# A fused linear-attention and MLP kernel: doubled powers of w taken one step later, w's column through ScalarE's queue, 11 dummies, the last copy in two halves

## The chip, the cores and the metric

The kernel runs on one core of a Trainium2 chip. The metric is device microseconds of one launch; lower is better. The time before is the median of three runs.

## The reference

Two steps follow one another. The first is a linear attention with a decaying state (4 batches, 8 heads, 768 positions, head width 48), the second an MLP with an unusual activation over the 3072 tokens:

```python
for t in range(S):
    cur = einsum('bhd,bhe->bhde', u[None] * k[t], v[t])
    y[:, :, t] = einsum('bhd,bhde->bhe', r[t], state + cur)
    state = w[None, :, :, None] * state + einsum('bhd,bhe->bhde', k[t], v[t])
x = y.transpose(0, 2, 1, 3).reshape(B * S, H * D)   # 3072 x 384
h = x @ w_in                                        # 384 x 2048
g = h * erf(softplus(h))
return g @ w_out                                    # 2048 x 384
```

## The kernel before

**Tiling.** The 768 positions of a batch are cut in chunks of 128, 24 chunks in all; four chunks make a block of 512 tokens, and there are six blocks. Inside a chunk the decay is taken out of the recurrence by scaling r with rising powers of w and k with falling ones, so that the chunk's scores are one matrix product A, masked, and the state is carried on by products with w to the 128th. The MLP then works on a block of 512 tokens and 128 hidden columns at a time: 96 steps (h, activation, output sum). Matrix products of the MLP are done in three pieces, high and low parts of both operands.

**Order.** Nothing is left to a scheduler. A string ORDER of short words is walked from left to right (lines 549 to 619), and each word issues one step on its engines: L loads a chunk, B builds the tables of powers (L179 to L185), J multiplies a chunk by them (L228), A is the score product (L317), V turns k (L249 to L261), P masks (L328), Y and D are the output and the state products (L346, L369), f and p the two MLP products (L425, L485), a to l the steps of the activation, O the output (L497 to L514), Z0a, Z0b and Z0c a count of columns of w that lie outside 0.7 to 0.97. An engine takes its instructions in this order and stands still when one has to wait.

**The start.** SyncE (SP) sends the loads; the first two are wc, w as a column (112 partitions by 4), and uc, the same for u (L77 to L80). The chunks' loads follow (L71, L75). VectorE clears a tile `warm`; ScalarE does one Tanh on it (L89), which loads its activation table; then TensorE does WARM = 16 dummy products of this tile into a spare accumulator (L95, L516, L719). Meanwhile VectorE makes the powers (L163 to L177): `wp[n]` is w to the 2^n (a square, L171) and its reciprocal (L172), and `pw` holds all powers from 0 to 63, doubled in length with each of six products (L176). The 64 powers times w to the 64th give the other half of the tables `wrk` (L184 on VectorE, plain copies on ScalarE, L182). The first chunk is multiplied by them at L230, and the first A follows. Pool clears and fills small tables beside it, `own` among them (L216 to L222), which takes w to the 128th.

**The count and the end.** The count's matmul (L527, two of 4 columns) sums flags in `bad`. A rare case of w outside its bounds is handled behind a branch on that count (L629 to L631), which every engine passes at the end. The last step's three output tiles (128 by 512 each) are copied out of their accumulators, tiles 0 and 2 by ScalarE (L506), tile 1 by VectorE (L504), and sent to memory by SP (L492), one transfer of 256 KB each.

Of the kernel before, what the change touches and what calls it, by code (L numbers as in the profile page):

```python
# [18 lines left out]
ALU = mybir.AluOpType  # L19
# [4 lines left out]
SHIFT = 256.0  # L24
# [5 lines left out]
P = 128  # L30
C = 128
D = 48
NPAIR = 4
PR = 112
NF = 16
NQ = 3
TB = 512
# [6 lines left out]
def body(ctx: ExitStack, tc: tile.TileContext, att, attn, wcol, ucol, u, win, wout, levels, outT):  # L44
    nc = tc.nc
# [31 lines left out]
    wc = const.tile([PR, NPAIR], F32, name="wc")  # L77
    nc.sync.dma_start(out=wc, in_=wcol)
    uc = const.tile([PR, NPAIR], F32, name="uc")
    nc.sync.dma_start(out=uc, in_=ucol)  # L80
    ub = const.tile([P, 384], F32, name="ub")
# [67 lines left out]
    H = C // 2  # L149
# [13 lines left out]
    wp = const.tile([PR, 8, 2, NPAIR], F32, name="wp")  # L163
# [3 lines left out]
    nc.gpsimd.memset(pw[:, 0, :, 0:1], 1.0)  # L167
    nc.vector.tensor_scalar(out=wp[:, 0, 0], in0=wc, scalar1=0.7, scalar2=0.97, op0=ALU.max, op1=ALU.min)
    for n in range(7):
        m = 1 << n  # L170
        nc.vector.tensor_tensor(out=wp[:, n + 1, 0], in0=wp[:, n, 0], in1=wp[:, n, 0], op=ALU.mult)  # L171
        nc.vector.reciprocal(out=wp[:, n, 1], in_=wp[:, n, 0])  # L172
        if n == 0:
            nc.vector.tensor_copy(out=pw[:, 1, :, 0], in_=wp[:, 0, 1])
        if n < 6:
            nc.vector.tensor_tensor(out=pw[:, :, :, m:2 * m], in0=pw[:, :, :, 0:m],  # L176
                                    in1=wp[:, n, :, :, None].to_broadcast([PR, 2, NPAIR, m]), op=ALU.mult)  # L177

    def tables(eng):  # L179
        for o, n in ((wr, 0), (wk, 1)):  # L180
            if eng is nc.scalar:
                nc.scalar.copy(out=o[:, :, 0:H], in_=pw[:, n])  # L182
            else:
                nc.vector.tensor_tensor(out=o[:, :, H:C], in0=pw[:, n],  # L184
                                        in1=wp[:, 6, n, :, None].to_broadcast([PR, NPAIR, H]), op=ALU.mult)  # L185
# [30 lines left out]
    own = const.tile([PR, NPAIR, 2], F32, name="own")  # L216
# [3 lines left out]
    nc.gpsimd.memset(top.rearrange("p n two -> p (n two)").bitcast(I32), 0)  # L220
    for r, hh in ((slice(0, D), 0), (slice(H, PR), 1)):
        nc.gpsimd.tensor_copy(out=own[r, :, hh], in_=wp[r, 7, 0])  # L222

# [264 lines left out]
    def put_out(n, e, blk=None):  # L488

        b = order[n][0]  # L490
        o = outT[b] if blk is None else outT[bass.ds(blk, 1)].rearrange("a p n -> (a p) n")
        nc.sync.dma_start(out=o[e * P:(e + 1) * P], in_=outs[n, e])  # L492

# [3 lines left out]
    def end(step, n, e):  # L497
        b, f = order[n]
        if step == "a":
            o = outs[n, e] = fp.tile([P, TB], F32, tag="s1" if n == NS - 1 and e == 2 else "o", name=f"o{n}_{e}")  # L500
            if (b, e) in part:
                nc.sync.dma_start(out=o, in_=part[b, e])
            elif b == NB - 1 and e == 1:
                nc.vector.tensor_scalar(out=o, in0=full[n, e], scalar1=SHIFT * SHIFT, scalar2=None, op0=ALU.mult)  # L504
            else:
                nc.scalar.mul(out=o, in_=full[n, e], mul=SHIFT * SHIFT)  # L506
# [42 lines left out]
    for i, x in enumerate(words):  # L549
# [22 lines left out]
        elif what == "B":  # L572
            tables(eng)
        elif what == "H":
            diagonals()
# [142 lines left out]

WARM = 16  # L719
LEAN = 8  # L720
# [55 lines left out]
l64 A23 p64x p64y a67 c66 d66 e66 b67 P230 P231 z67 g66 O631b O630b O632a p64z p65 f69 c67 h66 a68 b68 l66 S18c z68  # L776
c68 d68 e68 d67 e67 a69 g68 h68 g67 p66 Y23 Y22 X23a h67 X23b l68 X22a b69 X22b z69 l67 f70 f71 c69 d69 a70 b70 z70
e69 p67 c70 d70 a71 g69 b71 h69 l69 f72 a72 z71 c71 d71 e70 p68 p69 e71 g70 g71 h71 l71 b72 h70 z72 l70 f73 Z0b f74
p70 c72 a73 d72 e72 b73 a74 g72 Z0c z73 c73 h72 b74 d73 l72 p71 f75 O632b z74 e73 g73 c74 d74 h73 e74 a75 b75 g74 l73
# [78 lines left out]
```

## Time and profile before

| | us |
|---|---|
| median of three runs (500.76 to 502.0) | 500.99 |
| span of the profiled execution | 498.5 |
| TensorE (PE) busy in it | 489.1 |
| TensorE loading weights (PEld), beside it | 391.7 |
| ScalarE (ACT) busy | 390.6 |
| VectorE (DVE) busy | 334.2 |
| GpSimd (POOL) busy | 149.9 |

The profile gives the span of one execution, from its first to its last instruction; the runs' times take in what lies around it. Busy shares are averages over three stages: a start of some 8 us, the first attention chunks beside the fetching of weights, and the long stretch in which attention of later blocks and the MLP are woven together. TensorE is busy 98% of the span and makes up 92% of the chain of work that ended last, so the stages at both ends, where it is not busy, are to be read apart.

### The profile page before, as it was taken

The page shows a single profiled execution, that of the slowest core. Times are in us where ns is not written, and L with a number is a line of the kernel's source. Part 1 is how long each engine was busy: PE and PEld are TensorE (multiplying, and loading weights), DVE is VectorE, ACT ScalarE, POOL GpSimd, SP SyncE. Part 2 cuts the span into 40 slices and gives each one's busy share as a digit, 9 for nine tenths or more (in the row PEclk, how much of TensorE's full clock was granted, in tenths as well). Part 3 has the DMA queues.
Part 4 walks back from the last instruction along what each step waited for, and adds up shares of the span by engine and source line. Part 5 has one row for each costly group of instructions (what it writes and reads, how often), then busy time and mean ns, then how long its engine had stood idle before and what let it go on. Part 6 is the DMA issues. An engine that isn't in the chain of part 4 may idle for free.

```text
span 498.5 us, 10972 instructions
## 1 busy us (share of the span) xinstructions
PE 489.1 (98%) x4466; PEld 391.7 (79%) x4466; DVE 334.2 (67%) x584; ACT 390.6 (78%) x702; POOL 149.9 (30%) x132
## 2 busy tenths in 40 slices
PE   8999999999999999999999999999999999999995
PEld 4877888878778888888888878887878788888883
DVE  7999866667878966746766676786764544434552
ACT  2779999998976687877568875768877888978793
POOL 8749436016222735800067063361000000000000
PEclk9999999999999999999999999999999999999998
DMA  8965663328007603000440123231010000100001
GB/s 291 345 247 194 221 218 123 132 64 301 25 1 269 201 30 122 35 1 1 153 149 0 34 83 135 93 113 76 11 54 1 1 0 1 43 22 1 0 1 68
DMA packets 14136, 48.15 MB, mean 97 GB/s; under 512 B 1792, under 2 KB 2176, under 8 KB 14080
## 3 DMA queue, kind: packets, MB, share of 16 engines
q1 hardware_dynamic: 14080, 47.39, 26.8%
q8 instruction: 37, 0.61, 0.5%
q14 instruction: 19, 0.16, 0.1%
HBM read 41.09 MB, written 6.29 MB: 95 GB/s over the span
## 4 chain that ended last, share of the span: by engine, by line
PE 92%; DVE 4%; ACT 2%; issue 1%; DVEq 0%; ACTq 0%
PE h L425 39%; PE acc L485 39%; PE y L346 7%; PE A L317 4%; PE ds L369 1%; PE dummy L95 1%; DVE gl L468 1%; DVE am L325 1%; DVE s L457 1%; DVE s L441 1%; DVE wt L136 1%; PE kt L255 0%; ACT gh L463 0%; ACT L89 0%; ACT s L453 0%
## 5 line engine op out<-in xcount | busy, mean ns | idle before, releaser
L425 PE MATMUL h<-x,wih 128*128 128x512 f32 x576 | 182.8, 398 | 0.1
L425 PEld LDWEIGHTS h<-x,wih 128*128 128x128 f32 x576 | 107.1, 188 | 27.2 <-DVE s L457 0.6
L485 PE MATMUL acc<-gh,woh 128*128 128x512 f32 x288 | 115.2, 400 | 0.0
L485 PE MATMUL acc<-gl,woh 128*128 128x512 f32 x288 | 114.1, 396 | 0.3 <-DVE gl L468 0.2
L485 PE MATMUL acc<-gh,wol 128*128 128x512 f32 x288 | 113.9, 395 | 0.0
L425 PE MATMUL h<-x,wil 128*128 128x512 f32 x288 | 113.9, 395 | 0.0
L468 DVE TENSOR_TENSOR gl<-s,gh 128x512 fp32r<-128x512 f32 x96 | 71.3, 744 | 51.2 <-ACT gh L463 50.0
L457 DVE SCALAR_TENSOR_TENSOR s<-s,h 128x512 f32<-128x512 f32 x96 | 65.5, 684 | 49.0 <-ACT s L453 48.5
L441 DVE SCALAR_TENSOR_TENSOR s<-s,h 128x512 f32<-128x512 f32 x96 | 65.5, 685 | 34.8 <-ACT s L436 32.7
L445 ACT ACTIVATE s<-s 128x512 f32<-128x512 f32 x96 | 60.0, 626 | 23.5 <-DVE s L441 23.3
L432 ACT ACTIVATE s<-h 128x512 f32<-128x512 f32 x96 | 56.5, 590 | 26.5 <-PE h L425 26.2
L463 ACT CAST gh<-s 128x512 fp32r<-128x512 f32 x96 | 58.6, 613 | 20.5 <-DVE s L457 15.8
L485 PEld LDWEIGHTS acc<-gh,woh 128*128 128x128 f32 x288 | 54.1, 188 | 13.8 <-ACT s L445 0.2
L485 PEld LDWEIGHTS acc<-gl,woh 128*128 128x128 f32 x288 | 54.1, 188 | 13.7 <-DVE gl L468 1.2
L425 PEld LDWEIGHTS h<-x,wil 128*128 128x128 f32 x288 | 54.1, 188 | 13.0
L485 PEld LDWEIGHTS acc<-gh,wol 128*128 128x128 f32 x288 | 54.1, 188 | 12.9
L449 ACT ACTIVATE s<-s 128x512 f32<-128x512 f32 x96 | 60.3, 629 | 1.8
L436 ACT ACTIVATE s<-s 128x512 f32<-128x512 f32 x96 | 60.3, 629 | 1.7
L453 ACT ACTIVATE s<-s 128x512 f32<-128x512 f32 x96 | 60.0, 629 | 2.0
L536 POOL TENSOR_TENSOR att<-att,wrk 112x512 f32<-112x512 f32 x28 | 41.3, 1476 | 42.3 <-DMA att<-in_att_dram 39.9
L536 POOL TENSOR_TENSOR am<-idents,q 128x512 f32<-128x512 f32 x22 | 25.4, 1156 | 54.2 <-issue 24.3
L325 DVE COPY_PREDICATED am<-mask,A 64x128 f32<-64x128 uint32 (+2 forms) x108 | 38.0, 388 | 3.3 <-PE A L317 2.6
(88 smaller groups left out, 431.2 us busy)
## 6 DMA issues: line engine op xcount, KB each, us to landing
att<-in_att_dram SPq DMA_DIRECT2D x22, 608.0 KB, 5.6
att<-in_att_dram SPq DMA_DIRECT2D x24, 512.0 KB, 4.0
raw<-in_wout_dram SPq DMA_DIRECT2D x8, 768.0 KB, 5.6
raw<-in_win_dram SPq DMA_DIRECT2D x7, 768.0 KB, 4.7
out_dram<-o SPq DMA_DIRECT2D x18, 256.0 KB, 2.3
part<-o SPq DMA_DIRECT2D x6, 256.0 KB, 3.1
o<-part SPq DMA_DIRECT2D x6, 256.0 KB, 3.2
raw<-in_win_dram SPq DMA_DIRECT2D x2, 384.0 KB, 8.1
```

Of the source, the lines that this page charges most:

```text
L425: nc.tensor.matmul(out=h, lhsT=w[:, f, q, :], rhs=x[:, xi, q, :], start=k == 0, stop=k == 8)
L432: nc.scalar.activation(out=s1, in_=e["h"], func=AF.Tanh, bias=FB0, scale=FA0 * SHIFT)
L436: nc.scalar.activation(out=s1, in_=s1, func=AF.Tanh, bias=FB1, scale=FA1)
L441: nc.vector.scalar_tensor_tensor(out=e["s"], in0=e["s1"], scalar=FG / SHIFT, in1=e["h"], op0=ALU.mult, op1=ALU.add)
L445: nc.scalar.activation(out=s, in_=s, func=AF.Tanh, bias=FB2, scale=FA2 * SHIFT)
L449: nc.scalar.activation(out=s, in_=s, func=AF.Square, bias=FB3, scale=FA3)
L453: nc.scalar.activation(out=s, in_=s, func=AF.Square, bias=FB4, scale=FA4)
L457: nc.vector.scalar_tensor_tensor(out=s, in0=s, scalar=FC, in1=ff[n]["h"], op0=ALU.subtract, op1=ALU.mult, reverse0=True)
L463: nc.scalar.copy(out=e["gh"], in_=e["s"])
L468: eng.tensor_tensor(out=e["gl"], in0=e["s"], in1=e["gh"].bitcast(F32), op=ALU.subtract)
L485: nc.tensor.matmul(out=acc[e], lhsT=w[:, f, es], rhs=g, start=first and i == 0, stop=last and i == 2)
L536: i = nc.gpsimd.tensor_tensor(**kw)
```

## The change

Five edits are made together.

- wc and uc are sent by ScalarE's queue instead of SP's; in ScalarE's program they stand ahead of the Tanh.
- In the loop of powers, each product of `pw` uses the power of the step before, so that the next square and the next reciprocal stand between a reciprocal and the product that takes it. The seventh square, and Pool's copies into `own` that take it, move behind the tables (`powers`, called in word B).
- WARM is 11 instead of 16.
- The count's matmul (Z0b) moves from between two steps of f to right behind the y products of chunk 22 and 23.
- The last output tile is copied in two halves, columns 0 to 255 by ScalarE and 256 to 511 by VectorE, and its transfer is sent by ScalarE's queue.

```diff
     wc = const.tile([PR, NPAIR], F32, name="wc")
-    nc.sync.dma_start(out=wc, in_=wcol)
+    nc.scalar.dma_start(out=wc, in_=wcol)
     uc = const.tile([PR, NPAIR], F32, name="uc")
-    nc.sync.dma_start(out=uc, in_=ucol)
+    nc.scalar.dma_start(out=uc, in_=ucol)
...
+    def square(n):
+        nc.vector.tensor_tensor(out=wp[:, n + 1, 0], in0=wp[:, n, 0], in1=wp[:, n, 0], op=ALU.mult)
...
     for n in range(7):
-        m = 1 << n
-        nc.vector.tensor_tensor(out=wp[:, n + 1, 0], in0=wp[:, n, 0], in1=wp[:, n, 0], op=ALU.mult)
+        if n < 6:
+            square(n)
         nc.vector.reciprocal(out=wp[:, n, 1], in_=wp[:, n, 0])
         if n == 0:
             nc.vector.tensor_copy(out=pw[:, 1, :, 0], in_=wp[:, 0, 1])
-        if n < 6:
+        else:
+            m = 1 << n - 1
             nc.vector.tensor_tensor(out=pw[:, :, :, m:2 * m], in0=pw[:, :, :, 0:m],
-                                    in1=wp[:, n, :, :, None].to_broadcast([PR, 2, NPAIR, m]), op=ALU.mult)
+                                    in1=wp[:, n - 1, :, :, None].to_broadcast([PR, 2, NPAIR, m]), op=ALU.mult)
...
-    for r, hh in ((slice(0, D), 0), (slice(H, PR), 1)):
-        nc.gpsimd.tensor_copy(out=own[r, :, hh], in_=wp[r, 7, 0])
+
+    def powers():
+        square(6)
+        for r, hh in ((slice(0, D), 0), (slice(H, PR), 1)):
+            nc.gpsimd.tensor_copy(out=own[r, :, hh], in_=wp[r, 7, 0])
...
-        nc.sync.dma_start(out=o[e * P:(e + 1) * P], in_=outs[n, e])
+        (nc.scalar if n == NS - 1 and e == 2 else nc.sync).dma_start(out=o[e * P:(e + 1) * P], in_=outs[n, e])
...
+            elif n == NS - 1 and e == 2:
+                for eng, s in ((nc.scalar, slice(0, TB // 2)), (nc.vector, slice(TB // 2, TB))):
+                    if eng is nc.scalar:
+                        eng.mul(out=o[:, s], in_=full[n, e][:, s], mul=SHIFT * SHIFT)
+                    else:
+                        eng.tensor_scalar(out=o[:, s], in0=full[n, e][:, s], scalar1=SHIFT * SHIFT, scalar2=None, op0=ALU.mult)
...
         elif what == "B":
             tables(eng)
+            if eng is nc.vector:
+                powers()
...
-WARM = 16
+WARM = 11
...
-e69 p67 c70 d70 a71 g69 b71 h69 l69 f72 a72 z71 c71 d71 e70 p68 p69 e71 g70 g71 h71 l71 b72 h70 z72 l70 f73 Z0b f74
```

The last line holds the old place of Z0b; its new one is in the row above it of ORDER, between Y22 and X23a.

**What stands where.** Three places of the program, before and after; the line numbers after the first edited lines shift by up to 17. The first is the start: VectorE, from the third product of powers to the first product of a chunk. Here `wp` is the squares and reciprocals, `pw` the powers, `wrk` the tables, and "waits DVE" is a wait on an instruction of VectorE itself. Before:

```order
L176 TENSOR_TENSOR pw<-pw,wp 112x8x8 [waits DVE_49]
L171 TENSOR_TENSOR wp<-wp 112x4
L172 RECIPROCAL wp<-wp 112x4
L176 TENSOR_TENSOR pw<-pw,wp 112x8x16 [waits DVE_49]
L171 TENSOR_TENSOR wp<-wp 112x4
L172 RECIPROCAL wp<-wp 112x4
L176 TENSOR_TENSOR pw<-pw,wp 112x8x32 [waits DVE_49]
L171 TENSOR_TENSOR wp<-wp 112x4
L172 RECIPROCAL wp<-wp 112x4
L184 TENSOR_TENSOR wrk<-pw,wp 112x4x64 [waits DVE_49] x2
L230 TENSOR_TENSOR att_172<-att_172,wrk 112x1024 [waits DMAHW2_49,DVE_49,Activation_49]
```

After:

```order
L182 TENSOR_TENSOR pw<-pw,wp 112x8x8 [waits DVE_49]
L171 TENSOR_TENSOR wp<-wp 112x4 [waits DVE_49]
L177 RECIPROCAL wp<-wp 112x4
L182 TENSOR_TENSOR pw<-pw,wp 112x8x16 [waits DVE_49]
L177 RECIPROCAL wp<-wp 112x4 [waits DVE_49]
L182 TENSOR_TENSOR pw<-pw,wp 112x8x32 [waits DVE_49]
L190 TENSOR_TENSOR wrk<-pw,wp 112x4x64 [waits DVE_49]
L190 TENSOR_TENSOR wrk<-pw,wp 112x4x64
L171 TENSOR_TENSOR wp<-wp 112x4
L239 TENSOR_TENSOR att_164<-att_164,wrk 112x1024 [waits DMAHW1_49,DVE_49,Activation_49]
```

Before, a product takes the reciprocal that stands right ahead of it; after, the one that stands three rows ahead, and the last square has moved behind the tables.

And ScalarE in the same place, from its first instruction. Before:

```order
L853 UNCONDITIONAL_BRANCH [waits barrier_Pool_Activation_PE_DVE_SP_release]
L89 ACT_TABLE_LOAD
L89 ACTIVATE warm<-warm 128x1 [waits DVE_49]
L182 COPY wrk<-pw 112x4x64 [waits DVE_49,Pool_49]
L182 COPY wrk<-pw 112x4x64
```

After:

```order
L870 UNCONDITIONAL_BRANCH [waits barrier_Pool_Activation_PE_DVE_SP_release]
L78 DMA wc<-in_wcol_dram 112x4
L80 DMA uc<-in_ucol_dram 112x4
L89 ACT_TABLE_LOAD
L89 ACTIVATE warm<-warm 128x1 [waits DVE_49]
L188 COPY wrk<-pw 112x4x64 [waits DVE_49,Pool_49]
```

The two transfers stand ahead of the table load and of the activation for which TensorE's first dummy waits.

The second is TensorE around the count's matmul `cnt`; `h` is the first product of the MLP, `y` the output of the attention. Before:

```order
L425 MATMUL h_4713<-x_3546,wih 128x512 x2
L425 MATMUL h_4713<-x_3546,wil 128x512
L527 MATMUL cnt<-bad,wrk 1x4
L425 MATMUL h_4725<-x_3546,wih 128x512 [waits DVE_49]
L425 MATMUL h_4725<-x_3546,wih 128x512
```

After:

```order
L355 MATMUL y_4570<-am_1_4248,att_4067 32x128
L355 MATMUL y_4570<-am_0_4241,att_4067 32x128 x2
L355 MATMUL y_4570<-am_1_4248,att_4067 32x128 x5
L542 MATMUL cnt<-bad,wrk 1x4 [waits PE_49]
L434 MATMUL h_4614<-x_3541,wih 128x512 [waits DVE_49]
L434 MATMUL h_4614<-x_3541,wih 128x512
```

It stood between two h steps and stands between the last y matmul and an h step, with a wait on an earlier A matmul of TensorE itself.

The third is ScalarE and VectorE behind the last matmul; `o_2` is the last output tile, `fi` the count. ScalarE before:

```order
L463 CAST gh_5486<-s_95_5447 128x512 [waits DVE_49,PE_49]
L506 ACTIVATE o_0_5493<-acc_0_5047 128x512 [waits DMAHW5_49,PE_49]
L506 ACTIVATE o_2_5504<-acc_2_5083 128x512 [waits PE_49]
L629 TENSOR_LOAD fi [waits DVE_49]
L631 COMPARE_AND_BRANCH
```

ScalarE after:

```order
L472 CAST gh_5481<-s_95_5442 128x512 [waits DVE_49,PE_49]
L521 ACTIVATE o_0_5488<-acc_0_5042 128x512 [waits DMAHW5_49,PE_49]
L515 ACTIVATE o_2_5499<-acc_2_5078 128x256 [waits PE_49]
L501 DMA out_dram<-o_2_5499 128x512 [waits DVE_49]
L646 TENSOR_LOAD fi [waits DVE_49]
L648 COMPARE_AND_BRANCH
```

VectorE after:

```order
L477 TENSOR_TENSOR gl_5483<-s_95_5442,gh_5481 128x512 [waits Activation_49]
L519 TENSOR_SCALAR o_1_5497<-acc_1_5046 128x512 [waits DMAHW3_49,DMAHW4_49,DMAHW2_49,DMAHW6_49,DMAHW1_49,PE_49]
L517 TENSOR_SCALAR o_2_5499<-acc_2_5078 128x256 [waits Activation_49]
L646 TENSOR_LOAD fi [waits DVE_49]
L648 COMPARE_AND_BRANCH
```

ScalarE's copy has half the columns, a transfer has joined its queue, and VectorE has the other half, with a wait on ScalarE in front of it and none on TensorE.

## Rows read from the trace of the kernel before

**Rows 1.** Stretches: length, busy us (instructions) of each engine, granted clock, DMA share, GB/s.

```profile
core 0: us, PE busy (x) PEld busy (x) DVE busy (x) ACT busy (x) POOL busy (x), PEclk, DMA share, GB/s
8.49:26.60 18.11, 17.50 (x448) 15.12 (x447) 17.97 (x34) 10.99 (x31) 12.69 (x9) 1.00 0.90 336
52.30:492.60 440.30, 440.01 (x3579) 354.67 (x3579) 285.16 (x486) 354.26 (x630) 112.01 (x89) 1.00 0.22 77
```

**Rows 2.** Timeline of the start, ScalarE, SP and TensorE: start us, us, work, idle before.

```profile
0.82 1.28 ACT L89 ACT_TABLE_LOAD   x1 [0.82 <-PEq L846]
0.82 0.39 SPq L78 DMA_DIRECT2D wc<-in_wcol_dram  x1
1.28 0.41 SPq L80 DMA_DIRECT2D uc<-in_ucol_dram  x1
...
2.37 6.12 PE L95 MATMUL dummy<-warm 128*128 128x512 bf16 x16 [2.37 <-ACT warm L89]
```

**Rows 3.** Timeline of the start, VectorE.

```profile
2.48 0.17 DVE L168 TENSOR_SCALAR wp<-wc 112x4 f32<-112x4 f32 x1 [1.26 <-DMA wc<-in_wcol_dram]
...
4.37 0.23 DVE L176 TENSOR_TENSOR pw<-pw,wp 112x64 f32<-112x64 f32 x1
...
4.79 0.29 DVE L176 TENSOR_TENSOR pw<-pw,wp 112x128 f32<-112x128 f32 x1
...
6.60 1.23 DVE L230 TENSOR_TENSOR att<-att,wrk 112x1024 f32<-112x1024 f32 x1
```

**Rows 4.** The dummies: granted clock in their stretch, weight loads, and what follows them.

```profile
2.37:7.45 5.08, 5.08 (x13) 1.73 (x13) 4.53 (x25) 0.92 (x3) 4.65 (x12) 1.00 0.93 307
...
7.02 0.15 PEld L95 LDWEIGHTS <-warm 128*128 128x128 bf16 x1 [0.28 <-issue]
...
7.45 0.55 PEld L95 LDWEIGHTS <-warm 128*128 128x128 bf16 x3 [0.28 <-issue]
...
8.42 1.16 PE L317 MATMUL A<-att 48*128 48x128 f32 x16
...
9.62 0.69 DVE L330 TENSOR_TENSOR am<-A,mask 128x512 int32<-128x512 int32 x1
```

**Rows 5.** DMA issues at the start: transfer, issuer, KB, us from issue to landing.

```profile
wc<-in_wcol_dram SPq DMA_DIRECT2D x1, 1.8 KB, 1.6
...
att<-in_att_dram SPq DMA_DIRECT2D x1, 512.0 KB, 4.0
```

**Rows 6.** Timeline of TensorE behind chunk 22's y and at the count.

```profile
375.93 0.73 PE L425 MATMUL h<-x,wih 128*128 128x512 f32 x2
...
390.50 0.40 PE L425 MATMUL h<-x,wil 128*128 128x512 f32 x1
...
390.82 0.19 PE L527 MATMUL cnt<-bad,wrk 112*1 112x4 f32 x2
...
390.94 0.73 PE L425 MATMUL h<-x,wih 128*128 128x512 f32 x2
```

**Rows 7.** The tail: timeline, transfers of the output, VectorE's branch; first a narrower copy.

```profile
16.63 0.32 ACT L213 COPY wkn<-tp 128x192 f32<-128x192 f32 x1 [0.47 <-PE tp L208]
...
491.92 0.69 DVE L504 TENSOR_SCALAR o<-acc 128x512 f32<-128x512 f32 x1 [1.52 <-PE acc L485]
...
492.19 0.40 PE L485 MATMUL acc<-gh,wol 128*128 128x512 f32 x1
...
492.62 0.60 ACT L506 ACTIVATE o<-acc 128x512 f32<-128x512 f32 x1 [0.79 <-PE acc L485]
...
492.64 1.01 SPq L492 DMA_DIRECT2D out_dram<-o  x1
...
493.75 0.55 SPq L492 DMA_DIRECT2D out_dram<-o  x1
...
out_dram<-o SPq DMA_DIRECT2D x1, 256.0 KB, 3.0
...
DMA to landing us min/median/max: 2.0/2.3/6.5
...
L631 DVEq COMPARE_BRANCH  x1: 72/72/72, 492.6 to 492.6; - x1
...
L631 DVEq EVENT_SEMAPHORE  x1: 21/21/21, 495.5 to 495.5; - x1
```

More of the change, by code (lines that the diff above doesn't have):

```diff
@@ L776 @@
 l64 A23 p64x p64y a67 c66 d66 e66 b67 P230 P231 z67 g66 O631b O630b O632a p64z p65 f69 c67 h66 a68 b68 l66 S18c z68
-c68 d68 e68 d67 e67 a69 g68 h68 g67 p66 Y23 Y22 X23a h67 X23b l68 X22a b69 X22b z69 l67 f70 f71 c69 d69 a70 b70 z70
-e69 p67 c70 d70 a71 g69 b71 h69 l69 f72 a72 z71 c71 d71 e70 p68 p69 e71 g70 g71 h71 l71 b72 h70 z72 l70 f73 Z0b f74
+c68 d68 e68 d67 e67 a69 g68 h68 g67 p66 Y23 Y22 Z0b X23a h67 X23b l68 X22a b69 X22b z69 l67 f70 f71 c69 d69 a70 b70 z70
+e69 p67 c70 d70 a71 g69 b71 h69 l69 f72 a72 z71 c71 d71 e70 p68 p69 e71 g70 g71 h71 l71 b72 h70 z72 l70 f73 f74
 p70 c72 a73 d72 e72 b73 a74 g72 Z0c z73 c73 h72 b74 d73 l72 p71 f75 O632b z74 e73 g73 c74 d74 h73 e74 a75 b75 g74 l73
```

## The prediction

> **What bounds the kernel now.** I read the table of stretches first. From 52.3 us until the last matmul, TensorE is busy 440.01 of 440.30 us [rows 1]. Nothing that waits on another engine can shorten that stretch: an edit only moves it as a whole, or acts after it. From 8.5 to 26.6 us the two engines that count are both full, VectorE 17.97 and TensorE 17.50 of 18.11 us [rows 1], so an earlier start there is a rigid shift too. The change therefore has three places: the 8.4 us before the first attention matmul, one spot at 390.8 us where a tiny matmul stands, and the tail behind the last matmul. The timeline of each is read next, and I ask which wait ends last there.
>
> At the start two chains run side by side. VectorE's waits for wc, builds the powers, and ends in the first product `att<-att,wrk` at 6.60 us, over at 7.83 [rows 3]. TensorE's waits for ScalarE's activation table and warm-up, begins its dummies at 2.37 and is through with the 16 at 8.49 [rows 2]; the first A matmuls begin at 8.42 [rows 4]. Data were there 0.6 us earlier: **the dummies set the start**, not the powers. Behind it, VectorE's mask begins at 9.62, 0.04 us after the A matmuls' end at 8.42 + 1.16 = 9.58 [rows 4], so TensorE sets that too.
>
> **The powers.** Between two pw products VectorE now needs 0.42 us (4.37 to 4.79, [rows 3]): product, square, reciprocal, each taking the result of the one before, with a full wait between them. After the change the same instructions stand in the row, but each takes a result three places back. The count is the same (7 squares, 7 reciprocals, 6 products; the last square moves behind the tables, and Pool's two copies that take it are first needed by a later chunk's state), so the step falls to bare issue and execution; I estimate 0.30 us, from products of 0.23 to 0.29 us [rows 3] plus two short ones that overlap. Over five steps and the square that leaves the front this is 0.6 to 0.7 us: the first product of rows would begin at about 5.9 and end at 7.1 instead of 7.83. By itself this brings nothing, since the dummies cover it; it only becomes visible if they end before 7.1, which they do not (next).
>
> **Queue of wc and uc.** They leave SP's queue, where they stand at 0.82 and 1.28 [rows 2]. SP gets free two steps of 0.46, so the big loads are sent 0.92 us earlier; their landing limits nothing in [rows 3], where only wc's is waited for. But ScalarE now issues the two before its table load, 0.39 + 0.41 us and a gap [rows 2]. The table load begins 0.92 later, and with it the warm activation and the first dummy: 2.37 + 0.92 = 3.29.
>
> **Eleven dummies.** The clock column shows a grant of 1.00 while the dummies run [rows 4]; the level is seen in their pace. The weight loads come 0.43 us apart up to 7.45 (7.02, then 7.45) and take 0.15; the last three take 0.55 together, one per 0.22 [rows 4]. A dummy of 512 columns at 0.43 is 1.2 GHz, at 0.22 it is 2.4 GHz. So 12 of the 16 run at the low level, from 2.37 to about 7.5, then the clock rises. Eleven dummies from 3.29 at 0.43 end at 3.29 + 4.7 = 8.0, and A may begin at 8.05: 0.37 earlier. But they never reach the rise. If the rise stands as far behind the first dummy as it does now (2.37 to 7.45), it comes at 8.4, so A's first third runs at half pace: of 1.16 us [rows 4] about 0.15 is lost. Net **-0.2**. Bounds: -0.7 if the rise comes early and the dummies are short, +1.7 if the low level lasts through A, the kt matmuls and the second A. The row nearest to the chosen value is that of the dummies themselves.
>
> **The count matmul.** Now it stands between two h matmuls: h begins at 390.50, the count at 390.82, the next h at 390.94, so 0.44 us between h starts; of the next two the second begins 0.73 - 0.39 = 0.34 later [rows 6]. An undisturbed step is 0.22 to 0.23. The sum of the excess is 0.21 + 0.11 = 0.32; the two little matmuls themselves (0.19 busy together, some 0.12 of issue) are still paid. In its new place it waits only for an A matmul of TensorE itself, long done, and nothing queues up. Right behind the y matmuls a change of shape is paid anyway: there too, at 375.93, two h take 0.73 [rows 6]. I take **-0.2**, bounds -0.3 and 0.
>
> **The tail.** The last matmul ends at 492.19 + 0.40 = 492.59. ScalarE copies 512 columns in 0.60, to 493.22; SP is still sending the output before (492.64, 1.01 us), and sends the last at 493.75; it lands 3.0 later, 496.75, and the span ends 1.75 behind that [rows 7]. After the change the copy is in two halves, and ScalarE sends it, free of SP. The words "two halves" suggest two engines at once. The order of the instructions says otherwise: VectorE's half waits for ScalarE, whose half has written the same tile. So they follow one another: ScalarE's about 0.38 (between 0.32 for 192 columns and 0.60 for 512, [rows 7]), VectorE's about 0.41 (0.69 for 512, [rows 7]), with hand-overs of 0.03 (492.59 to 492.62) and 0.04 (as 9.58 to 9.62 above). The transfer is issued at 492.62 + 0.38 + 0.03 + 0.41 + 0.04 = 493.48: 0.27 earlier, all of it SP's queue and none of it the halves. Its landing: 3.0 now, right behind another output; the 18 outputs have 2.0 at least and 2.3 in the middle [rows 7]. I take 2.7, so 496.2. A second path ends near it: VectorE's branch on the rare case runs at 492.6, as its copy ends, and its next event comes at 495.5, 2.9 later [rows 7]; behind a half that ends at 493.44 that is 496.35. The later of both counts: **-0.4**. Bounds -1.25 (landing 2.0, branch hidden) and +0.2 (ScalarE's issue is long and pushes its own branch behind).
>
> The sum is -0.2 - 0.2 - 0.4 = **-0.8 us**: a span of 498.5 - 0.8 = 497.7. The median lies 500.99 - 498.5 = 2.5 above the profiled span, so **500.2 us**.
>
> **Rivals.** First: *the start gives nothing or costs a little*. wc is a tiny transfer of 1.8 KB that lands 1.6 us after its issue, while a 512 KB load takes 4.0 [rows 5]. Alone at the head of one queue it is ahead of everything; now the loads of att are sent at 0.82 from SP at the same moment, so wc can share engines with the first chunk. The price lies between 0 and 4.0 - 1.6 = 2.4; up to 0.7 + 0.3 of it is hidden (by the faster powers, and by the dummies' end at 8.0). The decisive point: wc landing after about 3.4. Beyond, each us goes into the start, and the 1.2 GHz stretch may be longer as well. With a start of +0.4 to +1.5 and the other terms halved: 500.6 to 502.0, say 501.0. The Trainium skill, "DMA: Bandwidth & Descriptors", section "Issuing engines are not separate DMA queues", says that transfers sent from different engines run on the same 16 DMA engines and interleave, so that another sender saves issue time alone. By that rule this rival is the case to expect, at about 501; no run here shows it yet, and the trace of before cannot, as all is sent by SP.
>
> Second: *all three gain more*. The clock rises as early as the dummies allow and A is not slowed (-0.4), the count is wholly hidden (-0.3), the last output lands in 2.0 to 2.3 with the branch out of the way (-0.9): -1.6 and a little, 499.0 to 499.5. For it speaks that 2.3 is the middle of 18; against it that the 3.0 was measured at just this place.
>
> Third, on the other side: *the clock stays low*. With 11 dummies the chip has seen five fewer than the 16, and none at the high level. If the engine's pauses behind them (A, then waits on masks) are enough to keep it at 1.2 GHz until the dense h matmuls come in at 26.6, the 17.50 us of TensorE work in between [rows 1] costs between half as much again (weight loads 0.15 against 0.10) and twice: +8.7 to +17.5. VectorE was full beside it, so nothing hides it: about 509. It decides where the rise has not come by about 14 us. Against it: TensorE is busy 17.50 of 18.11 there, as dense as the dummies were.
>
> That the change does not do what it says is part of the forecast: the halves are not parallel.
>
> **How the numbers follow.** The forecast, 500.2 with 499.5 to 500.6 of its own, has 0.50; the first rival 0.25; the second 0.19; the third 0.06. The range from 499.1 to 501.9 takes the first three nearly whole and leaves out the third and the ends. A measurement of this kernel can tell about 0.3%, 1.5 us: faster is under 499.5, slower over 502.5. Faster: the second rival, 0.19, and a little of the forecast's edge, 0.20. Slower: the third, 0.06, and the end of the first, 0.07. The rest, 0.73, is no difference.
>
> **What would show it.** In the timeline of the start: two issues on ScalarE at 0.82 and 1.28, the table load at about 1.74, the first dummy near 3.3, eleven of them with loads 0.43 apart and 0.15 long, A at about 8.05 with a longer busy time than 1.16; wc's wait on VectorE over by 2.5 (forecast) or after 3.4 (first rival); the first product of rows at about 5.9. The mask at 9.4 instead of 9.6, and the first h as much earlier. At the count: h starts 0.23 apart at that place, and one 0.34 behind y. In the tail: VectorE's half begins after ScalarE's has ended, ScalarE's transfer is issued about 0.9 behind the last matmul (1.16 now) and lands 2.7 later. I am wrong if the dummies don't set the start (A begins well before 8.0), if the halves overlap, or if the stretch between 8.5 and 52 us is not shifted rigidly.

## The result, and the profile after

The changed kernel is slower: 505.18 us median against 500.88 before, ratio 1.0091 (95% interval 1.0073 to 1.0108). The forecast was 500.2, a gain within the noise, with a range from 499.1 to 501.9. The loss of 4.3 us comes from two of the three places that the prediction looked at.

The two timelines, cut at four marks, say where (us; the marks are the first A, the first h, the last matmul's end and the span's end):

| stretch | before | after | difference |
|---|---|---|---|
| start to the first A matmul | 8.42 | 9.50 | +1.08 |
| first A to first h | 18.11 | 21.18 | +3.07 |
| first h to the last matmul's end | 466.06 | 465.52 | -0.54 |
| last matmul's end to the span's end | 5.91 | 7.10 | +1.19 |
| span | 498.5 | 503.3 | +4.8 |

The second stretch, before and after (columns as in [rows 1]):

```profile
8.42:26.53 18.11, 17.50 (x447) 15.12 (x446) 17.97 (x33) 10.92 (x31) 12.69 (x9) 1.00 0.91 338
```

```profile
9.50:30.68 21.18, 20.37 (x447) 17.83 (x447) 18.99 (x34) 11.00 (x31) 12.26 (x10) 0.84 0.69 248
```

The spans differ by more than the medians, since the profiled execution of the kernel before was one of its quicker ones: 498.5 us, where the middle span of some ninety runs of it beside the experiments is 499.3.

**The start.** Timeline of the changed kernel (columns as in [rows 2]):

```profile
0.82 1.33 SPq L71 DMA_DIRECT2D att<-in_att_dram  x3
0.83 0.41 ACTq L78 DMA_DIRECT2D wc<-in_wcol_dram  x1
...
1.74 1.28 ACT L89 ACT_TABLE_LOAD   x1 [1.74 <-PEq L863]
...
3.29 4.20 PE L95 MATMUL dummy<-warm 128*128 128x512 bf16 x11 [3.29 <-ACT warm L89]
...
4.87 0.17 DVE L168 TENSOR_SCALAR wp<-wc 112x4 f32<-112x4 f32 x1 [3.65 <-DMA wc<-in_wcol_dram]
...
6.66 0.34 PEld L95 LDWEIGHTS <-warm 128*128 128x128 bf16 x2 [0.28 <-issue]
...
8.22 1.23 DVE L239 TENSOR_TENSOR att<-att,wrk 112x1024 f32<-112x1024 f32 x1
...
9.50 1.57 PE L326 MATMUL A<-att 48*128 48x128 f32 x16 [2.01 <-DVE att L239]
```

The table load and the first dummy are 0.92 later, as forecast. But VectorE waits for wc until 4.87 instead of 2.48 [rows 3]. The powers themselves are shorter: 8.22 - 4.87 = 3.35 us from wc to the first product of the tables, 6.60 - 2.48 = 4.12 before. The dummies end at 3.29 + 4.20 = 7.49, so TensorE stands idle for 2.0 us, and the row of A names VectorE's product as what it waited for. A then takes 1.57 instead of 1.16 [rows 4].

The DMA view names the first cause. wc takes 4.0 us from issue to landing, 1.6 before [rows 5], at the same moment as SP's first chunk load:

```profile
att<-in_att_dram SPq DMA_DIRECT2D x1, 512.0 KB, 3.8
wc<-in_wcol_dram ACTq DMA_DIRECT2D x1, 1.8 KB, 4.0
```

The table of stretches names the second (columns as in [rows 1]; the granted clock is the number behind the bracketed ones):

```profile
6.69:10.11 3.42, 1.41 (x14) 0.80 (x14) 3.33 (x10) 0.92 (x3) 3.18 (x7) 1.00 1.05 419
10.11:16.93 6.82, 6.82 (x62) 6.00 (x64) 5.37 (x9) 0.54 (x2) 5.99 (x5) 0.50 0.67 263
16.93:30.68 13.75, 12.94 (x386) 11.22 (x375) 13.01 (x26) 10.46 (x29) 5.71 (x5) 1.00 0.68 233
```

Behind the gap of 2.0 us, when A has run for 0.6 us, the grant falls to 0.50, the 1.2 GHz level, for 6.82 us, and comes back to 1.00 (2.4 GHz) at 16.93. TensorE is busy in all of those 6.82 us, and its work goes at about half the pace of the higher level: the second A takes 2.08 us there, 1.16 before. From first A to first h its busy time is 20.37 us in the changed kernel, 17.50 before. The fall is not peculiar to the profiled execution: the mean grants of the four runs are 0.987 to 0.992. In every trace the grant falls in the tail too, but even the whole tail, 7.1 us, at half the clock would take only 0.007 off the mean.

**The count** did what it should. Behind y there is nothing left to pay: before, the h at 375.93 [rows 6] begins 0.99 behind the start of the last y group; after, the h at 379.89 begins 1.00 behind 378.89, with the count in between. So the 0.32 of [rows 6] is gone whole. Before, and after:

```profile
374.94 1.06 PE L346 MATMUL y<-am,att 128*32 128x128 f32 x32
```

```profile
378.89 1.06 PE L355 MATMUL y<-am,att 128*32 128x128 f32 x32
379.76 0.20 PE L542 MATMUL cnt<-bad,wrk 112*1 112x4 f32 x2
379.89 0.73 PE L434 MATMUL h<-x,wih 128*128 128x512 f32 x2
```

**The tail.** Timeline, the last transfer, and VectorE's branch:

```profile
495.80 0.40 PE L494 MATMUL acc<-gh,wol 128*128 128x512 f32 x1
496.24 0.38 ACT L515 ACTIVATE o<-acc 128x256 f32<-128x256 f32 x1 [0.80 <-PE acc L494]
496.65 0.42 DVE L517 TENSOR_SCALAR o<-acc 128x256 f32<-128x256 f32 x1 [0.42 <-ACT o L515]
497.11 0.38 ACTq L501 DMA_DIRECT2D out_dram<-o  x1
...
out_dram<-o ACTq DMA_DIRECT2D x1, 256.0 KB, 3.6
...
L648 DVEq COMPARE_BRANCH  x1: 72/72/72, 497.3 to 497.3; - x1
...
L648 DVEq EVENT_SEMAPHORE  x1: 21/21/21, 502.3 to 502.3; - x1
```

The halves follow one another and the transfer is issued 497.11 - 496.20 = 0.91 behind the last matmul, both as forecast. But it lands 3.6 later, at 500.7, and VectorE's branch takes 5.0 us (497.3 to 502.3) where it took 2.9 [rows 7] (3.0 by the trace's times in ns). It now ends last, 1.6 behind the landing.

### The profile page after: what moved, and what is told of

Read it like the earlier page. It is cut to its first block, busy times and chain, and to the rows that moved or that the text cites. A ratio compares the mean times of both kernels' runs of the same rounds, so it can differ in the third digit from the quotient of the medians.

```text
span 503.3 us, 10960 instructions
## 1 busy us (share of the span) xinstructions
PE 489.6 (97%) x4461; PEld 393.4 (78%) x4461; DVE 333.9 (66%) x585; ACT 389.9 (77%) x702; POOL 147.4 (29%) x132
## 4 chain that ended last, share of the span: by engine, by line
PE 89%; DVE 5%; ACT 2%; issue 1%; DVEq 0%; ACTq 0%
PE h L434 39%; PE acc L494 37%; PE y L355 7%; PE A L326 4%; PE ds L378 1%; DVE am L334 1%; DVE gl L477 1%; DVE s L450 1%; DVE s L466 1%; PE kt L264 1%; DVE wt L136 1%; ACT s L454 0%; ACT gh L472 0%; ACT s L462 0%; ACT s L458 0%
## 5 line engine op out<-in xcount | busy, mean ns | idle before, releaser
L477 DVE TENSOR_TENSOR gl<-s,gh 128x512 fp32r<-128x512 f32 x96 | 70.1, 731 | 50.6 <-ACT gh L472 49.4
```

The lines of the kernel that those rows point to most:

```text
L477: eng.tensor_tensor(out=e["gl"], in0=e["s"], in1=e["gh"].bitcast(F32), op=ALU.subtract)
```

## Experiments

The theory after the two traces: (A) wc on another queue shares the DMA engines with the chunk loads, lands 2.4 us later, and opens a gap in TensorE's work; (B) the gap costs the clock; (C) the halves together with ScalarE's sending make VectorE's branch late. The rivals are stated with each run. Times and ratios are against runs of the kernel before on the same chip, whose median there was 500.8 to 501.1. Differences to the changed kernel's 505.18 are taken from one set of runs to another.

**wc and uc by ScalarE, alone** (on the kernel before):

```diff
-    nc.sync.dma_start(out=wc, in_=wcol)
+    nc.scalar.dma_start(out=wc, in_=wcol)
-    nc.sync.dma_start(out=uc, in_=ucol)
+    nc.scalar.dma_start(out=uc, in_=ucol)
```

> The kernel before with one edit: wc and uc are sent by ScalarE's queue (16 dummies, old powers, old tail). Theory A, the queue: wc now shares the DMA engines with the chunks' loads that SP sends at the same moment, so it lands 4.0 us after its issue as in the changed kernel, not 1.6; the first product of powers' tables then begins at 4.87 + 4.12 = 9.0 instead of 6.60 and the first A at about 10.2 instead of 8.42; TensorE stands idle between the dummies' end at about 8.6 and then. That gives 500.9 + 1.8 = 502.7 if the clock holds through the gap, about 506 if it falls as in the changed kernel. Rival B, the eleven dummies: wc's later landing is hidden, the only cost is the first dummy at 3.29 instead of 2.37, and the time is at most 501.8.

503.01 us, ratio 1.0044 (1.0022 to 1.0065): slower by this one edit. wc lands 3.8 behind its issue, A begins at 10.08 (10.2 expected) behind 1.5 us without a dummy, as its timeline shows:

```profile
10.08 1.16 PE L317 MATMUL A<-att 48*128 48x128 f32 x16 [1.45 <-DVE att L230]
```

A takes 1.16, so in this execution the clock held through the gap. The first h comes at 28.59, 2.06 later than before, of which A's delay is 1.66. (One of the ten runs, 505.99 us, has a mean grant of 0.990, lower than the tail alone can make it, so the clock did not hold in all of them.) Theory A stands; the rival would have had 501.8 at most.

**wc and uc back on SP** (on the changed kernel): the same two lines the other way.

> The changed kernel with wc and uc back on SP's queue; all else as changed, 11 dummies among it. Theory A: wc lands by 2.45, the first product of the tables begins at about 5.9, A at about 7.2 right behind the dummies (2.37 + 4.7 = 7.1), and there is no gap; the start gains about 1 us and the tail still loses 1.2: 500.9 in all, 4.3 under the changed kernel. Rival B: eleven dummies are too few whatever wc does, the clock stays at its low level through the first chunks as in the changed kernel, first h 3 us later than A's start alone gives: about 504.

500.33 us, ratio 0.9971 (0.9949 to 0.9994), 4.9 under the changed kernel. A begins at 7.29 with 11 dummies and takes 1.16, and the grant does not fall before the first h:

```profile
7.29 1.16 PE L326 MATMUL A<-att 48*128 48x128 f32 x16 [0.22 <-DVE att L239]
```

Eleven dummies are enough when the gap behind them is as short as this. The tail still takes 7.2 us behind the last matmul.

**20 dummies** (on the changed kernel):

```diff
-WARM = 11
+WARM = 20
```

> The changed kernel with 20 dummies instead of 11, so that they last until A can begin (3.29, eight at 0.43, twelve at 0.22: about 9.4 against 9.50). Theory A with the clock as second part: A at 9.50 runs in 1.16 instead of 1.57, the clock is granted throughout, first h at 27.6 instead of 30.68, time 505.2 - 3.0 = 502.2. Rival: the low pace behind A has another cause (loads that arrive later, VectorE), and the time stays at 505.

502.54 us (502.2 expected), with wc as late as in the changed kernel (3.9). Two rows of its table of stretches:

```profile
8.26:10.14 1.88, 1.88 (x10) 0.69 (x8) 1.85 (x3) 0.00 (x0) 1.76 (x4) 1.00 1.01 417
10.14:28.25 18.11, 17.31 (x447) 15.20 (x447) 17.78 (x32) 11.07 (x31) 13.51 (x10) 1.00 0.77 277
```

A begins 0.64 later than in the changed kernel, since the dummies now end behind the data, and yet the first h comes 2.43 earlier (28.25 against 30.68): from A to h it is 18.11 again, as before. This separates the two parts of the start: the 3.07 us between A and h are the clock's, and the 1.08 us by which A itself was late are wc's.

**SP's first load held back** (on the changed kernel; a memset of the tile ahead of it):

```diff
...
     nc.vector.memset(warm, 0.0)
+    chunks[0] = apool.tile([P, AW], F32, tag="att", name="att0")
+    nc.vector.memset(chunks[0][:, 0:V0], 0.0)
```

> The changed kernel, with SP's first chunk load held back until about 2.3 us by a memset of that tile on VectorE (1.1 us behind the memset of the dummies' tile); wc and uc are still sent by ScalarE at 0.83, but now alone. Theory A, shared engines: wc lands 1.6 us after its issue again, VectorE's first instruction on it begins at about 2.5 instead of 4.87. Rival A2, ScalarE's queue is itself slower: wc still lands 4.0 later, at 4.8. By A the start is then set by the held load (2.35 + 3.8 = 6.2) and the first A begins at 7.5 to 8.0, before or right behind the dummies' end; by A2 at 9.5 as in the changed kernel.

```profile
0.82 0.39 ACTq L79 DMA_DIRECT2D wc<-in_wcol_dram  x1
...
2.31 1.33 SPq L72 DMA_DIRECT2D att<-in_att_dram  x3
2.47 0.17 DVE L171 TENSOR_SCALAR wp<-wc 112x4 f32<-112x4 f32 x1 [0.18 <-DMA wc<-in_wcol_dram]
...
wc<-in_wcol_dram ACTq DMA_DIRECT2D x1, 1.8 KB, 1.6
```

(Timeline and DMA view of this kernel.) Same queue, same issue, and 1.6 us again. So ScalarE's queue is not slow; what made wc late is the chunk loads sent beside it. That is the rule of the Trainium skill that the prediction drew on for its first rival ("DMA: Bandwidth & Descriptors", section "Issuing engines are not separate DMA queues": transfers of different engines run on the same 16 DMA engines and interleave); this run and the changed kernel's 4.0 agree with it. The first load was sent 1.5 us later and the kernel became faster by 4.2 (501.03; 1.0004, 0.999 to 1.0018, against before). A began at 8.05, at the edge of what was expected.

**The tail, alone, in parts** (four kernels, all on the kernel before). The whole edit of the tail:

```diff
+            elif n == NS - 1 and e == 2:
+                for eng, s in ((nc.scalar, slice(0, TB // 2)), (nc.vector, slice(TB // 2, TB))):
...
-        nc.sync.dma_start(out=o[e * P:(e + 1) * P], in_=outs[n, e])
+        (nc.scalar if n == NS - 1 and e == 2 else nc.sync).dma_start(out=o[e * P:(e + 1) * P], in_=outs[n, e])
```

> The kernel before with the change of the tail alone: the last copy in two halves, its transfer from ScalarE's queue. If the tail's longer time (7.1 us from the last matmul's end to the span's end against 5.9) comes from these edits: the transfer is issued 0.9 behind the last matmul and lands 3.6 later, VectorE's branch on the count takes 5 us instead of 3, and the time is 500.9 + 1.2 = 502.1. If it comes from elsewhere (what runs before it, chance): 5.6 us behind the last matmul as predicted, 500.5.

Then its second part alone (the sender), its first part alone (the halves), and the halves with senders exchanged, whose sender line is:

```diff
-        nc.sync.dma_start(out=o[e * P:(e + 1) * P], in_=outs[n, e])
+        (nc.scalar if n == NS - 1 and e == 1 else nc.sync).dma_start(out=o[e * P:(e + 1) * P], in_=outs[n, e])
```

> The kernel before with one edit of the tail: the last output's transfer is sent by ScalarE's queue; its copy stays whole on ScalarE. In the kernels with the whole tail, VectorE's branch comes 1.09 us behind the last matmul and takes 4.4 to 5.0 us, and the span ends 6.8 to 7.3 behind the last matmul, against 5.6 to 6.0. Theory H (the halves): VectorE is through at its old time here, its branch takes 3.0, and the end comes 5.3 to 5.9 behind the last matmul. Rival S (the sender): two queues send side by side, the transfer lands 3.6 or more after its issue and the branch takes 4 us or more wherever it stands; the end comes 6.5 to 7.3 behind.

> The kernel before with the other edit of the tail: the last copy in two halves, one after the other on ScalarE and VectorE, the transfer still sent by SP. Theory H (the halves): VectorE's branch comes 1.09 behind the last matmul, its instructions are fetched beside the last outputs, it takes 4.4 or more, and the end comes 6.5 to 7.3 behind the last matmul. Rival S (the sender): the branch takes 3.0 from 1.09 on, so 4.1, still before the landing at 4.2; the end comes 5.7 to 6.0 behind.

> The kernel before with the copy in two halves, and with the last two transfers' senders exchanged: tile 1's is sent by ScalarE, tile 2's, the last, by SP. Sent by SP alone, the halves' late branch of VectorE took 3.4 us; with the last transfer on ScalarE's queue 4.4 to 5.0. Theory Q (two queues at work beside the fetch of VectorE's instructions, whichever of them sends last): the branch takes 4.4 to 5.0 here too and the end comes 6.6 to 7.3 behind the last matmul. Rival (only a last transfer on ScalarE's queue does it): 3.4, and the end comes 5.6 to 6.0 behind.

What the traces gave, in us behind the last matmul's end (one execution each, from the trace's times in ns):

| kernel | copy | senders of tiles 1 and 2 | branch begins | branch takes | span ends |
|---|---|---|---|---|---|
| before | whole | SP, SP | -0.03 | 3.0 | 5.9 |
| sender only | whole | SP, ScalarE | -0.03 | 2.9 | 5.9 |
| halves only | halves | SP, SP | 1.29 | 3.4 | 5.7 |
| senders exchanged | halves | ScalarE, SP | 1.09 | 4.4 | 6.5 |
| whole edit alone | halves | SP, ScalarE | 1.09 | 4.7 | 7.3 |
| changed kernel | halves | SP, ScalarE | 1.08 | 5.0 | 7.1 |

The rows behind two of them, VectorE's branch with halves only and with senders exchanged:

```profile
L637 DVEq COMPARE_BRANCH  x1: 72/72/72, 495.2 to 495.2; - x1
L637 DVEq EVENT_SEMAPHORE  x1: 21/21/21, 498.6 to 498.6; - x1
```

```profile
L637 DVEq COMPARE_BRANCH  x1: 72/72/72, 494.7 to 494.7; - x1
L637 DVEq EVENT_SEMAPHORE  x1: 21/21/21, 499.2 to 499.2; - x1
```

Both simple theories fell: neither the halves alone nor the sender alone lengthens the tail. It takes a late branch and two queues at work beside it, whichever sends last; exchanged, it was 0.1 short of the end that had been named for that. The other traces agree. With the whole edit, in the runs with wc back, with 20 dummies and with the first load held, the branch begins at 1.09 and takes 4.35 to 4.74; with the tail of before, in four more runs, it begins at -0.02 or -0.03 and takes 2.88 to 3.09. Halves only and senders exchanged, the two rows that tell one queue from two, have one execution each and lie 1.0 us apart.

What the branch waits for stays open. The DMA view of the changed kernel shows what moves beside it. In its first 2.0 us these are packets of the two output queues alone; then come those of the instruction queues, and in the last 1.6 us no packet begins:

```profile
q1 hardware_dynamic: 151, 0.27, 37.4%
q10 hardware_dynamic: 131, 0.25, 34.3%
...
q14 instruction: 3, 0.02, 4.7%
q8 instruction: 1, 0.02, 4.4%
q10 hardware_dynamic: 13, 0.01, 2.5%
...
DMA packets 0, 0.00 MB, mean 0 GB/s; under 512 B 0, under 2 KB 0, under 8 KB 0
```

The first group is 497.3 to 499.3, the second 499.3 to 500.7, the third 500.7 to 502.3. That the instruction packets are VectorE's, held up by the outputs, is a guess from their time: no name shows it, and it does not account for the last 1.6 us. Against it stands the run with 20 dummies, in which an instruction packet moved 1.1 us behind the branch, beside the outputs, and the branch took 4.35 all the same.

In whole times all four are hard to tell from before: 502.14 (ratio 1.0014, 0.9991 to 1.0037) for the whole edit, 501.14, 501.24 and 501.12 for the others. The whole edit's span has another 1.1 us in its start that is not the tail's: VectorE's second product took 2.29 there instead of 1.22 (last section).

**11 dummies, alone** (on the kernel before):

```diff
-WARM = 16
+WARM = 11
```

> The kernel before with 11 dummies instead of 16, nothing else. The dummies end at 7.1 or a little before, the first product of the tables, unchanged, at 7.83; A begins at 7.87 instead of 7.9 to 8.4, after a gap of 0.8 us. If such a gap is too short to cost the clock: 500.9 - 0.3 = 500.6. If any gap costs it, as the 2.0 us one of the changed kernel did: +3, 503.5.

501.75 us, ratio 1.0024 (0.9998 to 1.0049); single runs between 499.8 and 505.8. In the profiled one TensorE had nothing for 0.67 us ahead of A, and the clock fell, as the table of stretches shows:

```profile
7.89 1.16 PE L317 MATMUL A<-att 48*128 48x128 f32 x16 [0.67 <-DVE att L230]
...
7.29:10.70 3.41, 2.81 (x32) 2.54 (x34) 3.38 (x5) 0.00 (x0) 2.09 (x1) 1.00 1.04 400
10.70:14.11 3.41, 3.41 (x53) 3.04 (x55) 3.41 (x7) 0.54 (x2) 3.02 (x4) 0.50 1.01 405
```

So neither expectation holds for all executions. A gap of 0.67 us cost the clock here; in the trace with halves only, behind 16 dummies, one of 0.65 did not, nor did the one of 1.45 in the run with wc and uc by ScalarE. The ten runs agree with that: their mean grants go from 0.989 to 0.999. Eleven dummies held where the data came soon behind their end: in the runs with wc back (a gap of 0.22) and with powers, 11 dummies and the count (0.54), 22 in all, the mean grant is 0.996 or more.

**The powers, alone** (on the kernel before, 16 dummies; the loop, `square` and `powers` of the change, nothing else):

```diff
...
-        if n < 6:
+        else:
+            m = 1 << n - 1
             nc.vector.tensor_tensor(out=pw[:, :, :, m:2 * m], in0=pw[:, :, :, 0:m],
-                                    in1=wp[:, n, :, :, None].to_broadcast([PR, 2, NPAIR, m]), op=ALU.mult)
+                                    in1=wp[:, n - 1, :, :, None].to_broadcast([PR, 2, NPAIR, m]), op=ALU.mult)
...
```

> The kernel before with the powers one step behind their squares, 16 dummies, all else as before. The first product of the tables begins at 5.9 instead of 6.60 and ends at 7.1; A then waits for the dummies alone and begins when they end, 7.6 to 8.5 by when the clock rises among them (7.88 to 8.42 in the runs of the old powers). Without fewer dummies the gain is 0 to 0.3 us: 500.7. If the powers alone carry the gain of the run with powers, 11 dummies and the count (499.5): 499.8.

500.20 us, ratio 0.9981 (0.9966 to 0.9996): between the two expectations. The first product begins at 5.83 instead of 6.60. In this execution the clock rose early and all 16 dummies ended at 7.28, so A began at 7.21 with no help from a smaller number:

```profile
5.83 1.22 DVE L239 TENSOR_TENSOR att<-att,wrk 112x1024 f32<-112x1024 f32 x1
...
7.21 1.16 PE L326 MATMUL A<-att 48*128 48x128 f32 x16
```

Its first h, though, comes only 0.08 earlier than before (26.45 against 26.53), and the two profiled spans are 498.6 and 498.5. Where the 0.9 us between the medians lie, these two traces do not show.

**Powers, 11 dummies and the count** (the changed kernel with wc, uc and the tail as before):

```diff
-    nc.scalar.dma_start(out=wc, in_=wcol)
+    nc.sync.dma_start(out=wc, in_=wcol)
-    nc.scalar.dma_start(out=uc, in_=ucol)
+    nc.sync.dma_start(out=uc, in_=ucol)
...
-        (nc.scalar if n == NS - 1 and e == 2 else nc.sync).dma_start(out=o[e * P:(e + 1) * P], in_=outs[n, e])
+        nc.sync.dma_start(out=o[e * P:(e + 1) * P], in_=outs[n, e])
...
-            elif n == NS - 1 and e == 2:
-                for eng, s in ((nc.scalar, slice(0, TB // 2)), (nc.vector, slice(TB // 2, TB))):
...
```

> The changed kernel without the two edits that I hold for its loss: wc and uc are back on SP's queue, and the last tile is copied and sent as before. What is left are the powers one step behind, 11 dummies and the count behind y. The first A begins at 7.3 as in the run with wc back, right behind the dummies (2.37 + 4.7), 1.1 earlier than before; the count saves 0.3; the end comes 5.9 behind the last matmul: 500.9 - 1.1 - 0.3 = 499.5, 0.8 to 1 us under the run with wc back. If either edit is innocent of its loss, the time stays at 500.3 or over.

499.50 us, ratio 0.9974 (0.9963 to 0.9985): the version that beats both, 1.3 under before and 5.7 under the changed kernel, and just the time expected. Its dummies and A in the timeline, and the stretch from A to the first h:

```profile
5.74 0.83 PE L95 MATMUL dummy<-warm 128*128 128x512 bf16 x3
7.10 1.16 PE L326 MATMUL A<-att 48*128 48x128 f32 x16 [0.54 <-DVE att L239]
...
7.10:26.23 19.13, 17.70 (x447) 15.27 (x447) 18.55 (x34) 11.03 (x31) 11.50 (x10) 1.00 0.90 346
```

A begins 1.32 earlier than before, the first h only 0.30: from A to h it is 19.13 instead of 18.11. VectorE's second product begins at 7.69 instead of 8.46, so the engine that is full there gained 0.77, not 1.32, and part of that is lost on the way (it waits 0.5 us for a chunk load at 11.1). The sum of the expectation came out right by luck, with an error in its middle: the start brought 0.3 there, and the rest lies behind the first h (its last matmul ends 0.75 earlier than before's) and in the tail (5.6 against 5.9, with the same code).

## Why the prediction was wrong

**The step that failed is the queue of wc and uc.** The prediction sent the big loads 0.92 us earlier, said of them that "their landing limits nothing", and went on with wc landing 1.6 us after its issue as before. With them beside it wc took 4.0, about as long as the big load (3.8), and VectorE's wait was over at 4.87 instead of 2.48. So the 2.4 us that stood as the upper end of the first rival (4.0 - 1.6) was the true price. It should have been the middle of the forecast and not the edge of a rival: the load that wc was to share the engines with had a row [rows 5]. The rival priced the start well, at +0.4 to +1.5 where A came 1.08 later; the cover that it took off was there (the powers saved 0.77, and the dummies had ended later than the data). What it lacked in its 501.0 was a price for the gap, and the tail.

**The clock** was the largest term, and in the wrong place. The prediction had it that eleven dummies "never reach the rise" and that A's first third is slow (0.15 us). The clock did rise among the eleven, at 6.69: the weight loads, one per 0.43 us until then, come two in 0.34 (row at 6.66 above). It fell again behind the gap, and stayed low for 6.82 us, at 3.07 us of time. With A's 1.08 the start cost 4.15, where the bound of the dummies' term was +1.7. The third rival had the mechanism, pauses that keep the level low, and priced it for the whole stretch up to 26.6 (509); the run with 20 dummies shows that the gap is the cause and 3.07 the size. First and third rival are one chain here, and the prediction gave them as alternatives, with no more than "the 1.2 GHz stretch may be longer as well" in the first: the late wc makes the gap, the gap takes the clock.

**The tail** was right in the order of its steps and wrong in sign. The halves in a row (0.38 and 0.42), the issue at +0.91 (0.89 forecast): right. The landing of 2.7 was 3.6. The branch was named as a second path that ends close by, at 2.9 us [rows 7]; it took 5.0, at a place where two output queues were at work. A duration taken from a row was moved to another place, with other traffic, and held to be the same. -0.4 became +1.19, over the bound of +0.2.

**What sets the stage behind A** was misread as well, though the loss does not come from it. The prediction read off the mask at 9.62 that "TensorE sets that too", and took an earlier A for a rigid shift of all behind it. But the mask also follows VectorE's own second product, 8.46 + 1.22 = 9.68. The run with the sender only tells the two apart, since its start is unchanged and its clock rose earlier. Two rows of before and of that run:

```profile
8.46 1.22 DVE L230 TENSOR_TENSOR att<-att,wrk 112x1024 f32<-112x1024 f32 x1
```

```profile
7.88 1.16 PE L317 MATMUL A<-att 48*128 48x128 f32 x16
...
9.61 1.28 DVE L330 TENSOR_TENSOR am<-A,mask 128x512 int32<-128x512 int32 x2
```

A began 0.54 earlier, the mask 0.01, and the first h came no earlier (26.61 against 26.53). So the dummies set A's start, but what goes on behind A hung on VectorE's row, and with it on the powers. In that trace an earlier A alone gained nothing.

**What held.** The powers: 0.77 us saved where 0.6 to 0.7 was worked out. The first dummy at 3.29. The count: all of 0.32, where 0.2 was taken. That TensorE's long stretch is only moved: 466.06 and 465.52, of whose 0.54 the count is 0.32. "The dummies set the start" holds for A in the profiled execution of before, but by chance: at 7.88 in the run with the sender only the data set it.

With the terms put right (+1.08, +3.07, +1.19, and -0.5) the sum is the 4.8 us of the spans.

## What to carry to other kernels

A small transfer on which a chain waits belongs at the head of a queue with nothing big sent beside it; moving it to an idle engine's queue takes away its place in line, not its competition. Cover work that keeps TensorE's clock up should last until the data are there: when it is shortened, or the data come later, the price can be not only the gap but a slow stretch behind it (3.07 us here, nothing in another execution). Before a start is called earlier, look for the engine that the stage behind it hangs on. And the time of a branch at the end of a kernel is a time beside certain traffic: when it is moved, read what the DMA engines do at its new place.

## What the hardware showed that was not expected

- The clock's rise among the same dummies comes at different times in different executions: 16 of them from 2.37 on, and the trace's record of the grant, which begins when the dummies' pace doubles, begins at 5.02 (powers alone), 6.03 (sender only) or 7.48 (before). The first A moves by it, and where the dummies end early a gap opens with the start unchanged too (0.65 us with halves only). Of some ninety runs of the kernel before, five have a mean grant of 0.990 to 0.993, lower than the tail alone can make it, at 503.1 to 504.9 us; of the 32 runs with the faster powers and wc on SP's queue none lies under 0.996. That the shorter gap is the reason was not tested.
- In all thirteen traces VectorE's second product of a chunk takes 1.22 us when it begins before Pool's product of a chunk, and 2.29 when Pool's is under way. In the run with halves only Pool began at 8.26 and VectorE at 8.65; in the run with the sender only Pool began at 8.57, behind VectorE's 8.47:

```profile
8.65 2.29 DVE L230 TENSOR_TENSOR att<-att,wrk 112x1024 f32<-112x1024 f32 x1
...
8.26 1.60 POOL L542 TENSOR_TENSOR att<-att,wrk 112x512 f32<-112x512 f32 x1 [1.52 <-DMA att<-in_att_dram]
```

```profile
8.47 1.22 DVE L230 TENSOR_TENSOR att<-att,wrk 112x1024 f32<-112x1024 f32 x1
...
8.57 2.25 POOL L536 TENSOR_TENSOR att<-att,wrk 112x512 f32<-112x512 f32 x1 [2.01 <-DVE att L247]
```

The first h was 1.0 us later in the three traces with the long product (27.64 or 27.65 against 26.53 and 26.61). With the faster powers VectorE's product begins at 7.69 to 7.88, ahead of Pool's in all three traces; that this is part of why the powers alone gain 0.9 us in the median was not tested.
